# The middle stage of an FFT long convolution: pairs of frequency groups on the two halves of the TensorE array

## The chip, the cores and the metric

The kernel runs on one core of one Trainium2 chip. The metric is the device time of one execution in microseconds. Before the change it was 375.13 us, the median of 3 runs (375.03 to 375.66).

## The reference, cut to what matters

Two sequence layers over 2048 steps and 1024 channels are computed and put side by side in one bf16 output of 2048 x 2048.

```
# A: a gated long convolution
kv  = shift_conv4(k, shift_k) * v                     # 4 taps, per channel
y   = irfft(rfft(kv, 4096) * rfft(ssm_k, 4096))[:2048] + kv * ssm_D
a   = q * y
# B: a diagonal complex state space layer
Bu  = x @ B_bar.T ;  h_t = Lam_bar * h_(t-1) + Bu_t   # 1024 complex states
b   = 2 * Re(h @ C.T) + x * Dskip
out = concat([a, b], -1)
```

The change is in A alone, in the product of the two spectra and the transforms on either side of it.

## The kernel before

**Layer A in three stages.** The 4096-point transform is split into 16 residues `n2` of the step number, a 128-point transform over the rest, and a 16-point transform across the residues.

Stage 1 makes `kv` for each `n2` on VectorE (`kvm`, `kva`, `kvb`, `kvc`), transforms it with the constant `F1t` (task `am`, L573), copies it out on ScalarE (`ae`, L580) and stores it into the DRAM tensor `Ys_kv` (`ast`). The filter takes the same way: transposes (`hT`, L595), `hm` (L612), `he` (L618), `hst` (L625), into `Ys_h`.

Stage 2 handles 32 groups of 4 frequencies; a load brings two groups (`lh` from `Ys_h`, `lk` from `Ys_kv`; a pair is called `gq`, a group in it `gi`). One group fills 128 partitions: real or imaginary part x 16 residues x 4 frequencies. Its steps, each over two halves `w` of the 1024 channels, are

- `sh`, `sk` (L642): one 128x128 matmul of 512 columns each, with the constant `W2` of this group; the result has the real part in partitions 0 to 63 and the imaginary part in 64 to 127;
- `she` (L650) and `ske` (L656): ScalarE copies out of PSUM into `hab[:, 0, :]` and `x16`;
- `sw` (L661, L662): two DMAs from SBUF to SBUF, one on SyncE's queue and one on GpSimd's, that write into `hab[:, 1, :]` the same values with the halves of the partitions exchanged;
- `pr` (L667): one VectorE multiply of 2048 elements in each partition, `x16` by both parts of `hab`;
- `sa` (L676): two 128x128 matmuls that add up in one PSUM bank (with the constants `Wa`, `Wb`), `sae` (L683): the copy out, and `vst` (L685): the store of a pair into the DRAM tensor `Vs`.

Stage 3 loads each residue of `Vs` (`vl`), transforms back with `Gt` (`a3`, L702), copies out (`a3e`, L708), multiplies by q (`qm`, L712) and stores (`ost`, L714). A residue holds rows of all groups, so no `vl` can run before the last `vst`.

**Layer B** runs beside it in 16 chunks of 128 steps: `U` (L462, 128 matmuls of 128 columns in each chunk), `ue` (L464), two rotations, a scan and a carry on VectorE (`r1` to `r4`, `sc`, `rc`, `cm`, `ca`), then `y` (L517, with the skip term at L522) and `ye` (L528).

**The order** is written out by hand in the string `ORDER`: a list of words, each a task with its numbers and the buffers that it takes (`p` a PSUM bank of eight, `a`, `b`, `m`, `w` buffers in SBUF). Each engine and each DMA queue executes its instructions in the order of this list, so a wait holds up what stands behind it on the same engine. The tasks of both layers are mixed in it, and PSUM has no bank that one task owns.

Of the kernel before, what the change touches and what calls it, by code (L numbers as in the profile page):

```python
# [22 lines left out]
NG = 32  # L23


def a_constants():
# [32 lines left out]
    W3 = np.stack([W2.reshape(128, NG, 128), Wa.reshape(128, NG, 128), Wb.reshape(128, NG, 128)], axis=2)  # L59
# [7 lines left out]
ld_w:a0a1 wb.0:p0 wb.3:p1 wbe.3 cl.2.0:b0 bl.2.1:b1 wb.2:p2 ld_par par_T:p3 bl.3.0:b2 p32 exp1 dve2 wb.6:p4 exp2 wbe.2 wbe.6 wb.1:p1 dve3 sm_pre sin0  # L67
tabA1:a0a2a3a4 cT.2.0:p3 bl.1.1:b3 bT.1.1:p2 bc.1.1 bl.0.0:b4 bT.0.0:p4 wbe.1 wbe.0 bT.2.1:p1 bc.0.0 bT.3.0:p0 bc.3.0 bl.0.1:b5 bT.0.1:p5 bc.0.1
bl.3.1:b6 wb.7:p4 cc.2.0 bl.1.0:b7 bT.1.0:p6 x.1:b8 bT.3.1:p7 bc.1.0 wb.4:p0 U.1.0.0:a5p5 wbe.4 x.3:b9 U.3.0.0:a6p3 bl.2.0:b0 bT.2.0:p6 dd U.3.0.1
x.0:b10 wb.5:p0 U.0.0.0:a7p2 wbe.7 bc.2.1 bc.2.0 bc.3.1 U.1.1.0:p6 U.1.1.1 U.1.0.1 U.0.1.0:p7 U.3.1.0:p1 U.0.0.1 wbe.5 sin1 tabA2 sin2 par_rest eo  # L70
kp.-1 kp.0 kvm.1:m0 ue.1.0 kp.1 kvm.2:m1 U.0.1.1 kva.1 U.3.1.1 ue.3.1 ue.1.1 bl.4.1:b5 ue.0.0 x.2:b2 U.2.1.0:p0 bT.4.1:p5 bc.4.1 bl.4.0:b6 bT.4.0:p1
bc.4.0 stt kvb.1:b6 kva.2 bl.5.1:b7 bl.7.0:b0 bT.5.1:p6 bT.7.0:p2 bl.5.0:b1 bT.5.0:p4 bc.5.0 U.2.0.0:a1p5 U.2.0.1 kp.-2 ue.0.1 ue.2.0 bl.6.0:b4
bT.6.0:p4 bc.7.0 kvm.0:m0 bc.6.0 bc.5.1 U.0.2.0:p7 x.4:b3 U.4.0.0:a4p5 bl.6.1:b11 bT.6.1:p2 cl.3.1:b12 bc.6.1 bl.7.1:b13 U.1.2.0:p1 x.5:b14 U.0.2.1
ue.0.2 kvb.2:b11 kva.0 bT.7.1:p6 bc.7.1 vp.0:a8 z2 cT.3.1:p2 cc.3.1 ld_F cl.3.0:b0 z1 U.0.3.0:p4 U.0.3.1 cl.1.1:b1 ld_G U.1.2.1 ue.0.3 U.1.3.0:p6
U.1.3.1 cT.3.0:p2 kvm.3:m1 ue.1.2 vp.1:a9 U.2.1.1 kvb.0:b12 ue.3.0 kvc.0 am.0.0:p7 ae.0.0:b0 U.4.0.1 ue.1.3 ue.4.0 am.0.1:p1 cc.3.0 kva.3 cl.2.1:b7
cT.2.1:p3 kvc.2 kvb.3:b13 am.2.1:p7 am.2.0:p4 ae.2.0:b7 ae.2.1 U.2.2.0:p6 r1.0:m0 r2.0:a0 cT.1.1:p5 U.2.3.0:p2 ae.0.1 cc.1.1 am.0.2:p4 ae.0.2:b1
am.0.3:p7 ue.2.1 ae.0.3 hl.1.0:a3 U.2.2.1 U.3.2.0:p1 ue.2.2 kvc.1 am.1.3:p4 am.1.2:p0 ae.1.2:b12 ast.0.1 U.3.3.0:p5 cl.1.0:b4 cT.1.0:p6 U.3.3.1 kvc.3
cc.2.1 ae.1.3 ue.3.3 am.2.3:p3 hl.0.0:a10 am.2.2:p0 ae.2.2:b4 U.3.2.1 ue.3.2 ae.2.3 sc.0.1 sc.0.0 hl.0.1:a2 hT.0.2:p5 U.2.3.1 hc.0.2:b11 ue.2.3
U.4.2.0:p1 hm.0.2.0:p3 he.0.2.0:b1 ast.2.0 cc.1.0 cl.0.0:b5 cx.7.1 hl.1.1:a7 hT.1.1:p5 r1.1:m0 cT.0.0:p2 ast.0.0 hc.1.1:b5 am.1.0:p0 cm.0 cx.5.0
r2.1:a9 hT.0.0:p3 hc.0.0:b0 U.4.2.1 ue.4.2 hT.1.0:p6 ast.1.1 hm.0.2.1:p5 hc.1.0:b12 ast.2.1 hm.0.2.2:p4 hm.0.2.3:p7 he.0.2.1 he.0.2.2:b11 U.4.3.0:p3  # L80
U.4.3.1 ue.4.3 cx.6.0 am.1.1:p6 cl.0.1:b7 cT.0.1:p5 cc.0.1 U.5.2.0:p4 ca.0 rc.1 r3.0:m1 sc.1.0 U.5.0.0:a5p3 sc.1.1 U.5.2.1 cm.1 r3.1:m0 ld_sd hd.0
hd.1 r4.1 cc.0.0 ae.1.0:b7 ae.1.1 U.5.0.1 ue.5.0 hst.0.2.0 hm.1.0.2:p6 he.1.0.2:b6 r4.0 hm.1.0.0:p0 ue.5.2 hT.0.3:p2 hm.1.0.1:p5 hc.0.3:b1 hm.1.0.3:p3
he.1.0.3 ca.1 he.1.0.0:b12 he.1.0.1 hl.2.1:a8 U.5.3.0:p1 r1.2:m0 y.1.0.0:p4 hm.0.3.0:p2 he.0.3.0:b4 ast.1.0 r2.2:a1 rc.2 sc.2.1 r1.3:m0 hst.1.0.1
hst.1.0.0 sc.2.0 hm.0.0.3:p3 U.5.3.1 ue.5.3 hm.0.3.1:p5 hm.0.0.2:p0 he.0.0.2:b7 y.1.0.1 hm.1.1.2:p1 he.0.0.3 he.0.2.3 hm.1.1.1:p0 hst.0.0.1 kp.2
kvm.4:m1 hT.0.1:p2 hm.0.0.1:p3 cm.2 hm.0.0.0:p7 he.0.0.0:b0 lw.0:w0 he.0.0.1 y.0.0.0:p6 he.1.1.2:b6 cx.6.1 hm.1.1.3:p7 r2.3:a6 he.1.1.3 hst.1.1.1
hst.0.0.0 ca.2 r3.2:m0 y.0.0.1 he.0.3.1 hm.1.1.0:p1 he.1.1.0:b5 he.1.1.1 hc.0.1:b12 y.0.0.2 hT.1.2:p5 kva.4 kvb.4:b0 kvm.5:m1 hm.0.3.2:p1 he.0.3.2:b7
hT.1.3:p7 hm.0.3.3:p0 he.0.3.3 hst.0.3.1 y.0.0.3 am.3.2:p1 hst.0.2.1 cx.4.1 cx.7.0 cx.4.0 cx.5.1 y.1.1.0:p2 hm.0.1.0:p0 hst.1.1.0 y.1.1.1 hc.1.2:b1
hm.1.2.3:p5 hst.0.3.0 he.0.1.0:b6 y.1.1.2 y.1.0.2 y.1.0.3 ye.1.0:b8 y.1.1.3 ye.1.1 hl.3.0:a2 yst.1 vp.2:a10 rc.3 hm.1.2.2:p0 he.1.2.2:b7 he.1.2.3 r4.2
hc.1.3:b11 am.3.3:p3 ae.3.2:b5 hst.1.2.1 y.0.1.0:p4 y.0.1.1 y.0.1.2 ye.0.0:b10 y.0.1.3 ye.0.1 kvc.4 ae.3.3 ast.3.1 hm.0.1.2:p6 hl.2.0:a3 hm.0.1.1:p1
he.0.1.1 hst.0.1.0 hm.1.3.2:p7 he.1.3.2:b4 hm.1.3.0:p5 he.1.3.0:b8 hm.1.3.3:p0 hm.1.2.1:p4 sc.3.0 hm.1.3.1:p2 kp.3 he.1.3.1 y.2.0.0:p3 hT.2.0:p1  # L90
hc.2.0:b11 kvm.6:m0 he.0.1.2:b7 hm.0.1.3:p5 he.0.1.3 he.1.3.3 hst.1.3.1 y.2.1.0:p7 am.3.1:p2 am.4.0:p1 y.2.1.1 ae.4.0:b12 y.2.1.2 am.3.0:p1 am.4.1:p0
ae.3.0:b5 U.4.1.0:p5 ae.3.1 kp.4 kva.5 hm.1.2.0:p1 hd.2 hm.2.0.1:p6 hm.2.0.2:p2 hst.0.1.1 U.4.1.1 ue.4.1 kvb.5:b13 ast.3.0 y.2.0.1 y.2.0.2 yst.0
hT.2.1:p5 y.2.0.3 lw.1:w1 sc.3.1 cm.3 ae.4.1 ast.4.0 he.2.0.2:b1 kvc.5 am.5.2:p2 he.1.2.0:b2 he.1.2.1 hst.1.2.0 r3.3:m1 hc.2.1:b4 ae.5.2:b7 hst.1.3.0
ca.3 r4.3 vp.3:a7 hm.2.0.3:p4 he.2.0.3 hst.2.0.1 kva.6 am.4.2:p1 hm.2.0.0:p0 ye.2.0:b11 y.2.1.3 ye.2.1 he.2.0.0:b10 am.4.3:p2 ae.4.2:b0 ae.4.3
hT.2.3:p4 hc.2.3:b12 he.2.0.1 hl.3.1:a9 hT.3.0:p3 hc.3.0:b2 am.5.0:p7 ae.5.0:b5 ast.4.1 am.5.1:p5 ae.5.1 ast.5.0 r1.4:m1 am.5.3:p0 ae.5.3 ast.5.1
kvb.6:b13 y.3.0.0:p1 y.3.0.1 hm.2.3.0:p4 vp.5:a0 hm.2.3.2:p6 he.2.3.2:b8 y.3.1.0:p2 y.3.1.1 r2.4:a4 x.6:b6 hst.2.0.0 hm.2.3.1:p5 he.2.3.0:b1 he.2.3.1
hT.3.2:p0 hd.3 hm.3.0.2:p6 rc.4 hm.3.0.3:p7 y.3.0.2 kvc.6 am.6.0:p5 hc.3.2:b9 hm.3.0.0:p4 he.3.0.2:b0 he.3.0.3 vp.4:a10 hm.2.3.3:p0 he.2.3.3 hst.2.3.0
hst.2.3.1 hm.3.0.1:p3 he.3.0.0:b2 he.3.0.1 am.6.2:p6 ae.6.2:b12 kvm.7:m1 kva.7 vp.6:a1 y.3.0.3 kvm.8:m0 hT.3.1:p0 am.6.3:p4 ae.6.3 kp.5 am.6.1:p7
hc.3.1:b7 kvb.7:b13 hm.2.1.3:p3 y.3.1.2 y.3.1.3 hm.2.1.2:p0 ye.3.0:b10 ye.3.1 hst.3.0.1 hT.2.2:p4 U.5.1.0:p1 hm.3.2.0:p2 yst.2 ast.6.1 ae.6.0:b1
ae.6.1 ast.6.0 sc.4.0 he.2.1.2:b5 he.2.1.3 vp.7:a6 hm.2.1.1:p5 hm.2.1.0:p7 hst.3.0.0 U.5.1.1 ue.5.1 U.6.0.0:a3p3 U.6.0.1 hm.3.2.1:p1 kvc.7 am.7.3:p0  # L100
he.2.1.0:b4 he.2.1.1 he.3.2.0:b8 ue.6.0 hst.2.1.1 am.7.2:p5 hm.3.2.3:p7 hc.2.2:b0 hst.2.1.0 sc.4.1 r3.4:m1 U.6.1.0:p2 U.6.1.1 he.3.2.1 hst.3.2.0 kva.8
ae.7.2:b12 ae.7.3 ast.7.1 hm.2.2.0:p1 hm.3.2.2:p4 am.7.0:p5 ae.7.0:b1 am.7.1:p3 ae.7.1 ast.7.0 hT.3.3:p6 he.3.2.2:b13 he.3.2.3 hm.3.1.2:p0 he.2.2.0:b9
hst.3.2.1 U.6.2.0:p5 kp.6 kvb.8:b11 hc.3.3:b2 yst.3 ue.6.1 cm.4 r4.4 y.4.0.0:p3 y.4.1.0:p7 hm.3.3.3:p1 kvc.8 am.8.3:p6 hm.3.3.2:p4 he.3.3.2:b4
am.8.2:p2 ae.8.2:b8 y.4.1.1 hm.2.2.1:p4 he.2.2.1 hst.2.2.0 U.6.2.1 he.3.3.3 ae.8.3 hm.2.2.2:p2 he.2.2.2:b1 hm.2.2.3:p4 he.2.2.3 hst.2.2.1 hm.3.1.3:p1
he.3.1.2:b13 he.3.1.3 y.4.1.2 hm.3.3.0:p6 he.3.3.0:b0 U.6.3.0:p2 ue.6.2 hm.3.3.1:p0 hm.3.1.0:p4 he.3.1.0:b10 hm.3.1.1:p1 he.3.1.1 kvm.9:m1 kvm.10:m0
kva.9 kvb.9:b12 U.6.3.1 hst.3.3.1 ue.6.3 he.3.3.1 lw.2:w2 hst.3.3.0 kva.10 ca.4 y.4.0.1 y.4.0.2 y.4.0.3 ye.4.0:b3 kvc.9 am.9.1:p0 am.9.2:p2 r1.5:m1
ast.8.1 x.9:b5 U.9.2.0:p1 am.8.0:p3 ae.8.0:b1 U.9.0.0:a5p4 U.9.0.1 ue.9.0 y.4.1.3 ye.4.1 am.8.1:p3 kvb.10:b9 r2.5:a10 hst.3.1.1 kvc.10 am.10.3:p5
kvm.13:m1 am.10.0:p4 am.10.2:p6 hst.3.1.0 U.9.3.0:p7 yst.4 ae.8.1 ast.8.0 ae.10.0:b11 U.9.3.1 ue.9.3 U.9.2.1 kp.7 kvm.11:m0 ae.10.2:b13 ae.10.3 kva.13
ue.9.2 x.8:b2 U.8.0.0:a4p4 kva.11 kvb.13:b10 U.8.2.0:p6 kvc.13 am.13.2:p1 ae.13.2:b8 am.13.0:p5 ae.9.2:b3 U.8.2.1 ue.8.2 x.11:b7 ae.13.0:b1 kvm.12:m1
am.9.3:p1 ae.9.3 kva.12 ast.9.1 am.10.1:p7 kvb.11:b9 ae.10.1 U.8.1.0:p3 am.13.3:p6 kvb.12:b0 kvc.11 ast.10.0 am.9.0:p2 am.13.1:p5 ae.13.1 ae.13.3  # L110
ast.13.1 x.7:b4 U.7.0.0:a2p1 lh.1:a9 U.7.1.0:p7 U.7.1.1 kvc.12 am.12.0:p6 am.12.3:p5 ae.9.0:b10 ae.9.1 U.8.0.1 ast.9.0 ast.10.1 ae.12.0:b12 ue.7.1
# [65 lines left out]
def full_kernel(ctx, tc, A_q, A_k, A_v, A_shift_k, A_ssm_k, A_ssm_D, B_x, B_Lre, B_Lim, B_Bre, B_Bim,  # L177
# [3 lines left out]
    nc = tc.nc  # L181
    P = 128
# [445 lines left out]
    def lw(gq):  # L628
        st["w", gq] = rtile(ring, "w", "wts", [P, GC, 3, P])
        spd(st["w", gq][:], W3v[:, gq * GC:(gq + 1) * GC, :, :])  # L630
# [15 lines left out]
    def she(g, w):  # L646
        if w == 0:
            st["hab", g] = k4("hab", [P, 2, D])
# [132 lines left out]
```

## Time and profile before

| | |
|---|---|
| median of 3 runs | 375.13 us |
| profiled execution, whole / its span | 374.92 us / 372.7 us |
| busy TensorE / VectorE / ScalarE / GpSimd | 352.9 / 328.2 / 280.5 / 110.5 us |
| DMA | 101.38 MB, 272 GB/s on the mean |
| `sw`: DMAs on SyncE's queue, on GpSimd's | 32 + 32 of 128 KB, 3.9 and 4.0 us from issue to landing |
| granted TensorE clock | 1.00 in nearly all of the span |

The span runs from the first to the last instruction on the core; 2.2 us of the profiled execution lie outside it. Busy time of TensorE counts a matmul from its start to its modelled end, and matmuls overlap in the array; the distance from one start to the next says what each one costs. About 1 in 80 matmul records is missing from this trace (3486 of 3529 are there), which shows as a double distance in some places.

### The profile page before, as it was taken

The numbers are of one execution on the slowest core, as the hardware profiler recorded it, in microseconds if no ns is written. First come the engines' busy times: TensorE is split into PE (matmuls) and PEld (weight loads), VectorE is DVE, ScalarE is ACT, GpSimd is POOL, SyncE is SP. The second block draws the span as 40 slices with busy tenths as digits, with TensorE's granted clock in tenths as the row PEclk, the third lists the DMA queues.
The fourth block names the chain that finished last, engine by engine and source line by source line (L and its number), as shares of the span: only waits on it lengthen the run. The fifth ranks groups of instructions, "written<-read, shape, count | busy, mean of one in ns | idle before, by whom it ended". The sixth has DMA issues, their size and how long they took to land.

```text
span 372.7 us, 8839 instructions
## 1 busy us (share of the span) xinstructions
PE 352.9 (95%) x3486; PEld 243.2 (65%) x3529; DVE 328.2 (88%) x335; ACT 280.5 (75%) x519; POOL 110.5 (30%) x188
## 2 busy tenths in 40 slices
PE   5999999998999889999999999999999999999894
PEld 3899999755666767878575557644574756646341
DVE  5999999999898989989999999989884989975960
ACT  4999999958789875878599869878878876155381
POOL 3000032584667676214111202202130232002134
PEclk9999999999999999999999999999999999999999
DMA  7999999899696789898899888897979899699656
GB/s 242 264 283 279 329 272 226 237 332 365 180 330 161 286 273 232 269 286 257 250 254 275 253 280 299 237 345 228 289 251 272 256 267 401 209 359 332 268 197 253
DMA packets 60100, 101.38 MB, mean 272 GB/s; under 512 B 31102, under 2 KB 33150, under 8 KB 60060
## 3 DMA queue, kind: packets, MB, share of 16 engines
q1 hardware_dynamic: 47868, 62.93, 60.1%
q0 software_dynamic: 12192, 37.90, 28.6%
q8 instruction: 27, 0.44, 0.5%
q14 instruction: 13, 0.11, 0.1%
HBM read 52.57 MB, written 33.55 MB: 231 GB/s over the span
## 4 chain that ended last, share of the span: by engine, by line
PE 69%; DMA 11%; ACT 6%; issue 6%; POOL 5%; DVE 1%; POOLq 0%; SPq 0%; ACTq 0%
PE ps_u L462 26%; PE ps_y L517 19%; PE ps_a L676 7%; PE ps_a L642 7%; DMA Ys_h<-ysbh 6%; POOL Ys_h L625 4%; DMA Ys_kv<-ysb 3%; PE ps_t L427 3%; PE ps_a L702 2%; PE ps_y L522 2%; ACT ot L708 2%; ACT ysb L580 1%; PE ps_a L573 1%; ACT ysbh L618 1%; PE ps_a L612 1%
## 5 line engine op out<-in xcount | busy, mean ns | idle before, releaser
L462 PEld LDWEIGHTS <-BT 128*128 128x128 bf16 x2048 | 120.2, 98 | 13.0 <-issue 1.5
L462 PE MATMUL ps_u<-xT,BT 128*128 128x128 bf16 x2048 | 126.9, 219 | 0.5
L517 PE MATMUL ps_y<-CT,h 128*128 128x512 bf16 x490 | 124.8, 379 | 0.7
L517 PEld LDWEIGHTS <-h 128*128 128x128 bf16 x512 | 45.8, 98 | 44.7 <-issue 0.7
L493 DVE TENSOR_TENSOR_SCAN h<-rtab,h 128x1024 bf16<-128x1024 f32 x32 | 71.9, 2279 | 0.2
L625 POOL DMA_DIRECT2D Ys_h<-ysbh x64 | 46.3, 725 | 26.8 <-ACT ysbh L618 23.1
L464 ACT CAST u<-ps_u 128x512 bf16<-128x512 f32 x64 | 38.3, 616 | 18.0 <-PE ps_u L462 17.4
L667 DVE TENSOR_TENSOR hab<-x,hab 128x2048 bf16<-128x2048 bf16 x32 | 38.4, 1221 | 11.7 <-ACT x L656 9.5
L650 ACT CAST hab<-ps_a 128x512 bf16<-128x512 f32 x64 | 35.9, 618 | 8.7 <-PE ps_a L642 8.4
L683 ACT CAST vsb<-ps_a 128x512 bf16<-128x512 f32 x64 | 35.3, 616 | 9.2 <-PE ps_a L676 6.9
L580 ACT CAST ysb<-ps_a 128x512 bf16<-128x512 f32 x64 | 36.0, 633 | 6.6 <-PE ps_a L573 3.3
L656 ACT CAST x<-ps_a 128x512 bf16<-128x512 f32 x64 | 37.0, 630 | 4.1 <-PE ps_a L642 4.1
L582 POOL DMA_DIRECT2D Ys_kv<-ysb x32 | 17.5, 550 | 74.5 <-ACT ysb L580 74.4
L618 ACT CAST ysbh<-ps_a 128x512 bf16<-128x512 f32 x64 | 34.6, 612 | 6.2 <-DMA Ys_h<-ysbh 3.7
L474 DVE TENSOR_TENSOR mt<-u,Z 128x4096 bf16<-128x4096 bf16 x16 | 36.4, 2282 | 2.8 <-ACT u L464 2.8
L474 DVE TENSOR_TENSOR mt<-h,Z 128x4096 bf16<-128x4096 bf16 x16 | 36.5, 2284 | 0.1
L528 ACT CAST yo<-ps_y 128x512 bf16<-128x512 f32 x32 | 18.9, 609 | 21.5 <-PE ps_y L517 18.0
L676 PE MATMUL ps_a<-hab,wts 128*128 128x512 bf16 x125 | 32.5, 379 | 0.2
L662 POOL DMA_DIRECT2D hab<-hab x32 | 16.9, 529 | 52.4 <-ACT hab L650 35.6
L553 DVE TENSOR_TENSOR mt<-kring,wbc 128x4096 bf16<-128x4096 bf16 (+3 forms) x16 | 30.0, 1883 | 0.1
L522 PE MATMUL ps_y<-Dd,xT 128*128 128x128 bf16 x128 | 28.0, 219 | 0.4
L612 PE MATMUL ps_a<-hT,F1t 128*128 128x256 bf16 x128 | 20.2, 272 | 2.4 <-ACT ysbh L618 1.1
(109 smaller groups left out, 420.9 us busy)
## 6 DMA issues: line engine op xcount, KB each, us to landing
Ys_kv<-ysb POOLq DMA_DIRECT2D x32, 256.0 KB, 4.0
Ys_h<-ysbh POOLq DMA_DIRECT2D x64, 128.0 KB, 4.2
l2h<-Ys_h SPq DMA_DIRECT2D x16, 512.0 KB, 5.3
l2k<-Ys_kv SPq DMA_DIRECT2D x16, 512.0 KB, 4.8
Vs<-vsb POOLq DMA_DIRECT2D x16, 512.0 KB, 5.0
vv<-Vs SPq DMA_DIRECT2D x32, 256.0 KB, 5.2
kring<-in_A_k_dram SPq DMA_DIRECT2D x8, 512.0 KB, 6.1
v<-in_A_v_dram SPq DMA_DIRECT2D x8, 512.0 KB, 4.3
```

The lines of the kernel that those rows point to most:

```text
L462: nc.tensor.matmul(pu[:, w, jl, :], BT[:, 2 * jp + jl, w, d, :], xT[:, d, :], start=(d == 0), stop=(d == ND - 1))
L464: E["ue"] = lambda i, jp: nc.scalar.copy(st["u", i][:, :, 2 * jp:2 * jp + 2, :], st["pu", i, jp][:])
L474: nc.vector.tensor_mul(m, s_, win(Z))
L493: nc.vector.tensor_tensor_scan(gf, rt1, gf, 0.0, ALU.mult, ALU.add)
L517: nc.tensor.matmul(py[:], h[:, 1 - w, j, :], CT[:, j, w, dh * 512:(dh + 1) * 512], start=(j == 0 and w == 0), stop=(j == NJ - 1 and w == 1))
L580: nc.scalar.copy(st["ysb", n2, cc][:, dh * 512:(dh + 1) * 512], st["pa", n2, w][:])
L618: nc.scalar.copy(st["yh", qd, n4, w // 2][:, :, w % 2, :], st["pa", qd, n4, w][:].rearrange("p (c d) -> p c d", c=2))
L625: gpd(Ys_h[cc, n0:n0 + 2, :, qd * DQ:(qd + 1) * DQ].rearrange("n k d -> k n d"), t_[:, cc, :, :])
L650: nc.scalar.copy(st["hab", g][:, 0, cols], pt[:])
L656: nc.scalar.copy(st["x16", g][:, w * 512:(w + 1) * 512], st["ps", "l2k", g, w][:])
L667: nc.vector.tensor_mul(hab[:], st["x16", g][:].unsqueeze(1).to_broadcast([P, 2, D]), hab[:])
L676: nc.tensor.matmul(pt[:], st["w", gq][:, gi, 1 + a, :], hab[:, a, w * 512:(w + 1) * 512], start=(a == 0), stop=(a == 1))
```

## The change

A pair of groups is now handled together. The weights of the forward transform are cut into 64 columns for the real and 64 for the imaginary part (`cc`), and the two groups of the pair go to the two halves of the partitions of one PSUM bank. Real and imaginary part then lie in the free dimension of the same partitions (`hh[:, cc, :]`), so every product of the complex multiply is made in place: `pr` multiplies the real part of x by both parts of h, then the imaginary part by both. The DMAs of `sw` are gone. The inverse transform takes 64 partitions of one group at a time, four products for each output, and the two groups write two banks.

```
-    W3 = np.stack([W2..., Wa..., Wb...], axis=2)                # [128, 32, 3, 128]
+    W3 = np.concatenate([W2.reshape(128, NG // 2, 2, 128), half(wa), half(-wa), half(wb)], axis=2)
...
-        st["w", gq] = rtile(ring, "w", "wts", [P, GC, 3, P])
+        st["w", gq] = rtile(ring, "w", "wts", [P, 5, P])
...
-    def s2(nm, g, w):
-        gq, gi = divmod(g, GC)
-        st["ps", nm, g, w] = ptile("ps_a", [P, 512])
-        nc.tensor.matmul(st["ps", nm, g, w][:], st["w", gq][:, gi, 0, :], st[nm, gq][:, gi, w * 512:(w + 1) * 512], start=True, stop=True)
+    def s2(nm, gq, cc, w):
+        pt = ptile("ps_a", [P, 512])
+        st["ps", nm, gq, cc, w] = pt
+        for gi in range(GC):
+            nc.tensor.matmul(pt[64 * gi:64 * gi + 64, :], st["w", gq][:, gi, 64 * cc:64 * cc + 64], st[nm, gq][:, gi, w * 512:(w + 1) * 512], start=True, stop=True)
...
-        spd(hab[0:64, 1, :], hab[64:128, 0, :])
-        gpd(hab[64:128, 1, :], hab[0:64, 0, :])
...
-        nc.vector.tensor_mul(hab[:], st["x16", g][:].unsqueeze(1).to_broadcast([P, 2, D]), hab[:])
+        if cc == 0:
+            st["pp", gq, 0] = k4("pp", [P, 2, D])
+            st["pp", gq, 1] = st["hh", gq]
+        nc.vector.tensor_mul(st["pp", gq, cc][:], st["xx", gq, cc][:].unsqueeze(1).to_broadcast([P, 2, D]), st["hh", gq][:])
...
-        for a in range(2):
-            nc.tensor.matmul(pt[:], st["w", gq][:, gi, 1 + a, :], hab[:, a, w * 512:(w + 1) * 512], start=(a == 0), stop=(a == 1))
+        for a in range(2):
+            wi = (2, 4, 4, 3)[2 * h + a]
+            for gi in range(GC):
+                rows = slice(64 * gi, 64 * gi + 64)
+                nc.tensor.matmul(st["ps", "v", gq, w][gi][:], st["w", gq][rows, wi, :], st["pp", gq, h][rows, a, w * 512:(w + 1) * 512],
+                                 start=(h == 0 and a == 0), stop=(h == 1 and a == 1))
```

The string `ORDER` is replaced by another one from its first word to its last, in which both layers stand in a new mixture. In it the half-array matmuls of several pairs stand together: 512 of them in 22 stretches that hold nothing of full size. For example, where stage 2 begins:

```
U.8.3.0:p4 U.8.3.1 ... sh.2.0.0:p6 she.2.0.0:a8 lh.0:a9 sh.0.0.0:p3 she.0.0.0:a11 sc.5.1 sh.2.0.1:p1 sh.0.0.1:p2 sh.1.0.0:p7 sh.1.1.1:p4
ast.11.1 x.10:b13 sh.2.1.1:p0 sh.0.1.1:p6 she.1.0.0:a12 sh.2.1.0:p3 ... U.11.2.0:p7
```

## The prediction

> **What bounds the kernel now.** First the head of the page: the span, and busy time by engine.
>
> ```profile
> span 372.7 us, 8839 instructions
> PE 352.9 (95%) x3486; PEld 243.2 (65%) x3529; DVE 328.2 (88%) x335; ACT 280.5 (75%) x519; POOL 110.5 (30%) x188
> ```
>
> TensorE's 95% could flatter it, since matmuls overlap. So next the timeline of TensorE alone, in a quiet stretch of stage 2 (start, length, instructions):
>
> ```profile
> 289.31 1.24 PE L517 MATMUL ps_y<-CT,h 128*128 128x512 bf16 x5
> 290.39 1.03 PE L642 MATMUL ps_a<-l2h,wts 128*128 128x512 bf16 x4
> 292.12 1.06 PE L462 MATMUL ps_u<-xT,BT 128*128 128x128 bf16 x16
> ```
>
> One matmul of 512 columns is listed in the groups with 379 ns, so five in 1.24 us start (1.24 - 0.379) / 4 = 0.216 us apart; sixteen of 128 columns (219 ns each) start (1.06 - 0.219) / 15 = 0.056 us apart. The same reading gives 0.109 for 256 columns. With these distances the whole program costs TensorE: U 2048 x 0.056 = 114.7; y 512 x 0.216 = 110.6 and its skip term 128 x 0.056 = 7.2; sh and sk 128 x 0.216 and sa 128 x 0.216 = 55.3; am and a3 64 x 0.216 each = 27.6; hm 128 x 0.109 = 14.0; 320 transposes at 0.056 to 0.062 = 18.7; the eight of L413 about 3.1. Sum 351.2 us. The first matmul starts at 4.5 and the last ends at 367.3 us, so the span is 4.5 + 351.2 + 11.6 of waits and slow starts + 5.4 after the last matmul. TensorE sets the time; nothing else has to be cheap, only early enough.
>
> Third, where the 11.6 us lie: the table by stretch (us; busy TensorE, its weight loads, VectorE, ScalarE, GpSimd, clock, DMA share, GB/s), cut at the stages, and the list of what TensorE waited for.
>
> ```profile
> 4.00:77.00 73.00, 71.59 (x1048) 64.41 (x1053) 69.81 (x111) 66.91 (x113) 12.47 (x19) 1.00 1.05 276
> 77.00:138.00 61.00, 56.03 (x490) 37.79 (x496) 57.81 (x53) 48.04 (x86) 39.61 (x59) 1.00 0.84 275
> 172.00:330.00 158.00, 156.90 (x1315) 96.39 (x1334) 144.80 (x115) 118.13 (x232) 30.11 (x56) 1.00 0.89 277
> 330.00:373.00 43.00, 35.32 (x211) 17.88 (x212) 23.99 (x27) 21.14 (x40) 11.27 (x21) 0.99 0.75 270
> ```
>
> ```profile
> PE ps_a L702 <- ACT ot L708: 1.8, 1, 1.8
> PE ps_a L573 <- ACT ysb L580: 1.4, 2, 0.9
> PE ps_a L612 <- ACT ysbh L618: 1.1, 1, 1.1
> PE ps_a L612 <- ACT yo L528: 1.0, 1, 1.0
> PE ps_a L573 <- DVE mt L560: 0.8, 1, 0.8
> ```
>
> With three smaller ones these waits make 7.4 us (the 4.5 before the first matmul apart); the rest is the slow clock of the first 6 us of matmuls. They belong to stage 1 and the end. The stretch 172 to 330, in which nearly all of stage 2 runs, has 156.9 busy of 158, and no wait of TensorE there is listed. That is the main reading: the change works where TensorE waits for nobody.
>
> **What is removed.** 64 DMAs of 128 KB and their issues: 32 x 0.467 = 14.9 us on SyncE's queue, 32 x 0.529 = 16.9 us on GpSimd's, 8.4 of 101 MB. Who waited for them, and for the step before:
>
> ```profile
> POOL hab L662 <- ACT hab L650: 35.6, 19, 3.4
> DVE hab L667 <- ACT x L656: 9.5, 5, 4.0
> DVE hab L667 <- DMA hab<-hab: 2.1, 2, 1.2
> ```
>
> The exchange cost VectorE 2.1 us of waiting and TensorE none, since U and y lay over it. GpSimd's 35.6 us held up the stores behind it on its queue, again under TensorE's work. Gain on the path: 0. The weights shrink from 192 to 160 KB a load, under the same cover: 0. What is late next for pr is ScalarE (the 9.5 us row).
>
> **What is unchanged.** she, ske, sae: 64 copies of about 0.62 us each; pr 32 x 1.22 us. Each stays as wide as it was. But pr now needs six copies of a pair, not four copies of one group; and sa holds two PSUM banks from its first half (h = 0) to its second and to their copies. An sa that waits holds back the U and y behind it.
>
> **What is added, on TensorE.** 256 full matmuls become 512 halves, in 256 pairs on disjoint halves of the array. No row of this trace shows a pair. The near end is 0.216 us a pair (each half still streams 512 columns, so a gain is excluded); the far end is two full ones, 0.432, 256 x 0.216 = 55.3 us more. I take the near end, because the distances above follow the columns streamed alone (56, 109, 216 ns) and the two halves share no cell of the array; plus 5 ns for the second issue, which is what lies between a load and its matmul in the next view (11.80 and 11.81): 256 x 0.005 = 1.3 us. [...]
>
> The loads double too, to 512 of half size. The row 172 to 330 has 156.9 us of matmuls and 96.4 us of loads in 158 us, all of full height: loads lie under running matmuls of the same rows. So I cost them at 0; unhidden, 256 column-half loads at 0.056 (a load and a matmul of 128 columns fit into that) would be 14.3 us. [...]
>
> Changing the form of the array has a price in this trace: L413 uses one row (a 32-row form) between full ones.
>
> ```profile
> 11.43 0.44 PE L427 MATMUL ps_t<-ident,ld 128*128 128x128 bf16 x5
> 11.80 0.09 PEld L413 LDWEIGHTS <-ones 1*128 1x128 bf16 x1
> 11.81 0.39 PE L413 MATMUL ps_a<-hk,ones 1*128 1x512 bf16 x1
> 12.12 0.28 PE L427 MATMUL ps_t<-ident,ld 128*128 128x128 bf16 x2
> ```
>
> The fifth L427 starts at 11.43 + 4 x 0.056 = 11.65, L413 0.15 later instead of 0.056; the next one 0.32 after L413 instead of 0.216. Six such places read singly give 95 to 102 ns. The program before changes form 7 times, the new one 49 times (rows, columns, full): 42 x 0.098 = 4.1 us, in a stretch without slack.
>
> **The new order.** It can move TensorE's waits both ways. Counting in both orders, over the 130 us of TensorE work of stage 2, how often a PSUM bank is taken again within 1.3 us of TensorE work after its last matmul: 23 of 212 before, 40 of 212 after; in the part of stage 1 where the waits are, 11 of 114 and 10 of 110. The half-array stretches fill banks faster (0.216 us each) than ScalarE empties them (0.62). Bounds: -7.4 us (all listed waits go) and +10.5 (17 further tight places at one copy of 0.62). I take 0, since 23 tight places cost nothing in stage 2 before.
>
> Sum: 4.1 + 1.3 = 5.4 us. Span 372.7 + 5.4 = 378.1, profiled execution 374.92 + 5.4 = 380.3, median 375.13 + 5.4 = **380.5 us**. A measurement of this kernel can tell about 0.2% (0.75 us) from no change.
>
> **Rivals.** (1) *The order wins back more than the forms cost*: faster. TensorE waits 7.4 us in stage 1 and the end, where the new order differs too, and fewer DMAs can free ScalarE's buffers earlier (5 waits, 3.7 us, for Ys_h stores). If all go, 380.5 - 7.4 = 373.1; without the 1.3 for pairs 371.8. It decides from 6.2 us regained. Against it: those waits are for stage 1, which the removed DMAs don't touch. Chance 0.23; another 0.06 that both cancel within 0.2%.
> (2) *Loads are not hidden, or stretches starve on PSUM banks*: 380.5 + 14.3 = 394.8, or 380.5 + 10.5 = 391. For it: 40 tight places. Chance 0.09.
> (3) *The halves don't run side by side*, so that the change doesn't do what it says: 380.5 + 55.3 - 1.3 = 434.5. One kind alone (columns or rows): about 407. Chance 0.09.
>
> **The numbers.** My forecast, pairs side by side and forms paid for, has 0.53 and its own range 376 to 386. Faster 0.23, same 0.06, slower 0.53 + 0.09 + 0.09 = 0.71. The range runs from 371.5 (rival 1 at its full price) to 395 (rival 2), and leaves out rival 3 and little else.
>
> **What would show it.** Right: in L642 and L676 two starts some ns apart, then 0.216 us to the next pair; about 0.1 us lost at each change of form; sum of TensorE's distances near 357; DVE's and POOL's hab rows gone, and the stretch of stage 2 longer by some 5 us. Wrong: starts 0.216 apart inside a pair (rival 3); starts of pairs 0.27 apart, or TensorE waiting for ACT copies of L650 to L683 (rival 2); TensorE's listed waits below 2 us (rival 1). A changed span with unchanged waits and 351 us of distances would refute the price of the forms.

## The result, and the profile after

The changed kernel takes 390.47 us (median of 4 runs, 386.12 to 394.29) where the kernel before takes 375.39 (375.03 to 377.81) beside it: a ratio of 1.035, with a 95% interval of 1.024 to 1.045. It is slower by some 15 us. The ratio leaves out the longest run, which is over 1.5% above the fastest. The profiled execution took 391.46 us, its span is 389.7 (before: 374.92 and 372.7), and the 17.0 us between the spans are what has to be found.

The head of its page answers to the first lines shown of before:

```profile
span 389.7 us, 9237 instructions
PE 363.3 (93%) x3785; PEld 244.9 (63%) x3785; DVE 332.3 (85%) x335; ACT 278.1 (71%) x519; POOL 93.0 (24%) x156
```

TensorE has 256 matmuls more (the page of before lacks the 43 records that are missing there) and 10.4 us more of busy time, while its share fell from 95 to 93%. Part of the loss is therefore work and part is time without work. GpSimd has its 32 instructions less.

The timeline of TensorE alone, where a stretch of half-array matmuls begins (start, length, instructions):

```profile
194.19 0.59 PE L524 MATMUL ps_y<-CT,h 128*128 128x512 bf16 x2
194.72 0.41 PE L650 MATMUL ps_a<-l2h,wts 128*64 128x512 bf16 x2
194.96 0.38 PE L650 MATMUL ps_a<-l2k,wts 128*64 128x512 bf16 x2
195.17 0.38 PE L650 MATMUL ps_a<-l2h,wts 128*64 128x512 bf16 x2
195.39 1.25 PE L650 MATMUL ps_a<-l2k,wts 128*64 128x512 bf16 x10
196.56 0.62 PE L469 MATMUL ps_u<-xT,BT 128*128 128x128 bf16 x8
```

Each of the first three L650 rows is a pair. Two matmuls of 0.38 us that ran one behind the other would show 0.216 + 0.38 = 0.6 us, as the L524 row of two does; these show 0.38 to 0.41. Single records give starts of 194.715 and 194.718, so 3 ns lie inside the pair, and the next pair follows after 0.24, then 0.21 and 0.22 us. Ten in 1.25 us are five pairs 0.216 apart. The two column halves do run at once.

The groups by shape (busy, mean ns) give 384 and 377 ns for one half-array matmul, as for a full one of 512 columns; only the distance between starts tells that two share it:

```profile
L650 PE MATMUL ps_a<-l2h,wts 128*64 128x512 bf16 x128 | 20.3, 384 | 0.0
L680 PE MATMUL ps_a<-pp,wts 64*128 64x512 bf16 x128 | 19.7, 377 | 0.0
```

Then the table by stretch, cut at the stages of the new order (us; busy TensorE, its loads, VectorE, ScalarE, GpSimd, clock, DMA share, GB/s):

```profile
5.00:77.00 72.00, 67.25 (x992) 60.10 (x992) 65.05 (x108) 61.00 (x103) 8.85 (x15) 1.00 1.04 264
77.00:150.00 73.00, 70.15 (x663) 48.50 (x662) 68.55 (x59) 54.98 (x99) 44.13 (x65) 1.00 0.80 247
150.00:183.00 33.00, 30.32 (x447) 26.41 (x445) 28.29 (x30) 24.61 (x49) 13.14 (x22) 1.00 0.73 208
183.00:320.00 137.00, 136.03 (x1275) 77.19 (x1272) 127.40 (x100) 110.81 (x222) 11.43 (x22) 1.00 0.67 219
320.00:390.00 70.00, 59.58 (x422) 32.61 (x420) 41.10 (x39) 25.43 (x49) 12.87 (x24) 0.95 0.73 254
```

The stretch of stage 2, 183 to 320, is as tight as before by this measure. The idle time has grown in stage 1, and there in the first row: 4.75 us against 1.41 before in the like row. The next two rows have 5.5 us, and before it was 5.9 from 77 to 172: 4.97 in the row 77 to 138 shown ahead and 0.9 in the one behind it:

```profile
138.00:172.00 34.00, 33.10 (x431) 26.66 (x436) 29.84 (x30) 25.00 (x50) 13.84 (x23) 1.00 0.89 251
```

The list of what TensorE waited for in the changed kernel names the waits:

```profile
PE ps_a L619 <- ACT hT L607: 3.6, 2, 3.3
PE ps_a L580 <- DVE mt L567: 2.7, 1, 2.7
PE ps_a L619 <- ACT ysb L587: 1.5, 1, 1.5
PE ps_a L580 <- ACT ysbh L625: 0.7, 1, 0.7
...
PE ps_a L680 <- DVE hh L670: 0.5, 2, 0.4
```

The chain of waits leads back from the 3.3 us wait to a store:

```profile
52.58 9.14 DMA Ys_kv<-ysb
...
61.80 0.42 ACT ysb L587
...
63.36 1.83 ACT hT L607 x2
...
65.73 0.27 PE ps_a L619
```

The buffer `ysb` came free when a store that took 9.14 us had landed. ScalarE's copies stood behind that, hT behind them, and the matmuls of L619 last.

The last place is the end. The table by stretch once more, for the last 13.7 us:

```profile
376.00:380.00 4.00, 4.00 (x22) 1.85 (x20) 1.90 (x3) 1.20 (x3) 2.36 (x5) 1.00 0.87 319
380.00:384.40 4.40, 0.35 (x2) 0.00 (x0) 0.00 (x0) 0.59 (x1) 0.54 (x1) 0.89 0.47 175
384.40:389.70 5.30, 0.00 (x0) 0.00 (x0) 0.00 (x0) 0.00 (x0) 0.00 (x0) 0.50 0.00 0
```

For 5.3 us no engine works and no DMA moves a byte. What fills 4.5 of them is an instruction of GpSimd's sequencer, which busy time leaves out: the closing DRAIN. Its row in the view by source line (least, median and largest ns, first and last start), before and then after:

```profile
L776 POOLq DRAIN  x3: 51/99/3701, 368.2 to 372.4; - x3
```

```profile
L780 POOLq DRAIN  x3: 51/112/7653, 381.2 to 389.4; - x3
```

Before, this DRAIN ended 0.7 us after the last store had landed (371.9 and 371.2 us) and the span 1.5 us after; now it is 5.3 us (388.9 and 383.6) and 6.1.

Measured from start to start of TensorE's matmuls, the 17.0 us divide as follows.

| | before | after | more |
|---|---|---|---|
| span's start to first matmul | 4.5 | 5.1 | 0.6 |
| first matmul to last matmul | 362.4 | 374.9 | 12.5 |
| of it: 44 changes of form at half-array matmuls | | | 4.2 |
| of it: pairs over 0.216 us | | | 0.7 |
| of it: waits inside half-array stretches | | | 3.2 |
| of it: waits at matmuls of full size | 9.7 | 13.7 | 4.0 |
| last matmul to the span's end | 5.8 | 9.7 | 4.0 |

The middle rows leave 0.4 us of slow clock and roundings. The 44 changes are 19 stretches entered and left, with six turns between column and row halves inside them; the stretches are 19 in the trace, and not the 22 that are named with the change.

### The profile page after: what moved, and what is told of

The parts are those of the page before. It is cut to its first block, busy times and chain, and to the rows that moved or that the text cites. A ratio compares the mean times of both kernels' runs of the same rounds, so it can differ in the third digit from the quotient of the medians.

```text
span 389.7 us, 9237 instructions
## 1 busy us (share of the span) xinstructions
PE 363.3 (93%) x3785; PEld 244.9 (63%) x3785; DVE 332.3 (85%) x335; ACT 278.1 (71%) x519; POOL 93.0 (24%) x156
## 3 DMA queue, kind: packets, MB, share of 16 engines
q0 software_dynamic: 10656, 33.71, 24.0%
## 4 chain that ended last, share of the span: by engine, by line
PE 51%; ACT 14%; issue 12%; DVE 10%; DMA 9%; POOL 2%; POOLq 0%; ACTq 0%; DVEq 0%
PE ps_y L524 18%; PE ps_u L469 15%; PE ps_a L680 4%; PE ps_a L650 4%; DMA Ys_h<-ysbh 4%; ACT hh L657 3%; PE ps_a L619 3%; PE ps_a L580 3%; ACT xx L663 3%; DVE mt L560 2%; DMA Ys_kv<-ysb 2%; ACT vsb L687 2%; DMA out_dram<-ot 2%; DVE mt L567 2%; POOL out_dram L718 1%
## 5 line engine op out<-in xcount | busy, mean ns | idle before, releaser
L524 PE MATMUL ps_y<-CT,h 128*128 128x512 bf16 x512 | 127.0, 379 | 0.3 <-ACT ot L712 0.2
L469 PE MATMUL ps_u<-xT,BT 128*128 128x128 bf16 x2048 | 124.7, 219 | 0.6 <-ACT BT L445 0.3
L469 PEld LDWEIGHTS <-BT 128*128 128x128 bf16 x2048 | 118.4, 98 | 10.5 <-issue 4.1
L524 PEld LDWEIGHTS <-h 128*128 128x128 bf16 x512 | 45.2, 98 | 45.0 <-issue 2.4
L625 ACT CAST ysbh<-ps_a 128x512 bf16<-128x512 f32 x64 | 35.6, 616 | 16.9 <-PE ps_a L619 6.6
L689 POOL DMA_DIRECT2D Vs<-vsb x16 | 8.5, 534 | 122.8 <-ACT vsb L687 96.7
L657 ACT CAST hh<-ps_a 128x512 bf16<-128x512 f32 x64 | 36.0, 649 | 2.3 <-PE ps_a L650 2.2
L687 ACT CAST vsb<-ps_a 128x512 bf16<-128x512 f32 x64 | 34.2, 694 | 3.3 <-PE ps_a L680 3.3
L663 ACT CAST xx<-ps_a 128x512 bf16<-128x512 f32 x64 | 35.8, 660 | 0.6 <-PE ps_a L650 0.6
L619 PE MATMUL ps_a<-hT,F1t 128*128 128x256 bf16 x128 | 20.5, 272 | 5.6 <-ACT hT L607 3.6
L712 ACT CAST ot<-ps_a 128x512 bf16<-128x512 f32 x32 | 17.4, 606 | 10.7 <-PE ps_a L706 6.3
L670 DVE TENSOR_TENSOR pp<-xx,hh 128x2048 bf16<-128x2048 bf16 x16 | 19.4, 1220 | 6.0 <-ACT xx L663 3.5
```

The costliest lines, as they stand in the source:

```text
L469: nc.tensor.matmul(pu[:, w, jl, :], BT[:, 2 * jp + jl, w, d, :], xT[:, d, :], start=(d == 0), stop=(d == ND - 1))
L524: nc.tensor.matmul(py[:], h[:, 1 - w, j, :], CT[:, j, w, dh * 512:(dh + 1) * 512], start=(j == 0 and w == 0), stop=(j == NJ - 1 and w == 1))
L625: nc.scalar.copy(st["yh", qd, n4, w // 2][:, :, w % 2, :], st["pa", qd, n4, w][:].rearrange("p (c d) -> p c d", c=2))
L657: nc.scalar.copy(st["hh", gq][:, cc, w * 512:(w + 1) * 512], st["ps", "l2h", gq, cc, w][:])
L663: nc.scalar.copy(st["xx", gq, cc][:, w * 512:(w + 1) * 512], st["ps", "l2k", gq, cc, w][:])
L687: nc.scalar.copy(st["vsb", gq][:, gi, w * 512:(w + 1) * 512], st["ps", "v", gq, w][gi][:])
```

## The experiments

Three theories stood after the first look. By the first (A in the expectations), the loss has two sources: the half-array matmuls, and an order in which TensorE waits for others; without the halves 4 to 6 us come back. By the second (B), the half-array matmuls are all of it, and without them the time comes back to some 376 us. By the third (C), their price lies in waits that would be there anyway, and nothing comes back. A further question was what the removed exchange is worth by itself. The chip's runs of the kernel before had medians of 376.32, 374.58 and 376.22 us in the three sets that follow; each ratio is against its own set.

### The change again, and the change with full matmuls

The changed kernel was run once more in the first set.

> The changed kernel once more, as the base of the others. Four runs so far lay between 386.1 and 394.3 us, those of the kernel before within 0.7 us but for one. Theory A (the new order leaves TensorE more waits for stores to land, and a heavier burst of stores at the end): the median stays near 390 and the spread of several us comes back, since the landing of stores varies. Theory B (a fixed price of the half-array matmuls): the same median, and a spread near that of the kernel before.

It took 392.18 us (389.14 to 397.14), ratio 1.038 [1.030, 1.047]: the same median within the noise, and the same wide spread.

Then the 512 halves became 256 matmuls of full size at the same places of the same order, with the same copies and products around them. The two groups are mixed in the sums, so the values are others.

```
-        for gi in range(GC):
-            nc.tensor.matmul(pt[64 * gi:64 * gi + 64, :], st["w", gq][:, gi, 64 * cc:64 * cc + 64], st[nm, gq][:, gi, ...], start=True, stop=True)
+        nc.tensor.matmul(pt[:], st["w", gq][:, cc, :], st[nm, gq][:, cc, ...], start=True, stop=True)
...
-            for gi in range(GC):
-                ...
+            nc.tensor.matmul(st["ps", "v", gq, w][a][:], st["w", gq][:, wi, :], st["pp", gq, h][:, a, ...], start=(h == 0), stop=(h == 1))
```

> The changed kernel with its order, banks, copies and DMAs, but each pair of half-array matmuls is one full 128x128 matmul of 512 columns (half of the products of the middle stage are left out). 256 matmuls instead of 512, form changes 5 instead of 49. Theory A: the price of the forms alone comes back, 44 x 0.095 = 4.2 us, and some 0.7 us of the pairs, so 4 to 6 us below the changed kernel, near 385; the rest stays with the order. Theory B: all the loss is in the half-array matmuls, so near 376. Theory C: the drains lie in waits that would be there anyway, so within 1 us of the changed kernel.

It took 390.34 us (388.7 to 393.37), ratio 1.037 [1.030, 1.044]. Changes of form and pairs, 4.9 us of TensorE's time by the table above, are gone, and the median came down by 1.8 us beside the run of the changed kernel, which the spreads don't tell from nothing. The second theory falls. Between the first and the third these medians don't decide: the first's own figure, 385 us, was missed by 5. In the two profiled executions the way from first to last matmul fell from 374.9 to 372.7 us, so 2.2 of the 4.9 us came through. Part of the rest is found again as waiting: at 50 places this kernel's TensorE waits 18.2 us, against 16.9 in the changed kernel (13.7 + 3.2).

```profile
PE ps_a L580 <- ACT ysbh L625: 2.5, 2, 1.6
PE ps_a L619 <- ACT hT L607: 2.2, 2, 2.0
PE ps_a L619 <- ACT ysb L587: 1.9, 2, 1.6
PE ps_a L677 <- DVE hh L669: 1.5, 4, 0.6
```

The table by stretch of the same kernel shows what one such wait can bring after it (the clock stands behind the five engines and ahead of the DMA share):

```profile
60.00:62.40 2.40, 0.49 (x9) 0.37 (x7) 0.69 (x3) 1.39 (x3) 1.09 (x2) 1.00 1.23 223
62.80:66.20 3.40, 3.40 (x25) 2.60 (x24) 3.33 (x4) 2.77 (x6) 0.35 (x1) 0.51 1.11 327
66.20:70.00 3.80, 3.80 (x36) 2.60 (x35) 3.77 (x3) 1.43 (x4) 1.11 (x2) 0.99 0.70 272
```

TensorE was busy 0.49 of 2.4 us, and for the 3.4 us after that its clock was 0.51. That is 25 matmuls where the following 3.8 us hold 36, and costs some 1.7 us over the wait itself (an estimate, 3.4 x 0.49). The profiled execution of the changed kernel has no such window, so this one is the greater part of what the full matmuls did not bring in these two traces, and it does not come in every execution.

The repeat of the changed kernel shows this best, for its profiled execution is the one of 397.14 us. It has three such windows, behind waits near 62, 123 and 158 us. This is the first of them, and the stretch ahead of it:

```profile
60.83:64.24 3.41, 1.15 (x21) 1.03 (x19) 1.20 (x4) 2.69 (x5) 1.09 (x2) 1.00 1.27 224
64.24:67.66 3.42, 3.42 (x25) 2.77 (x25) 3.35 (x5) 2.54 (x5) 0.00 (x0) 0.50 1.00 350
```

Three windows cost some 5 us (3 x 1.7 by the same estimate), and from first to last matmul this execution takes 6.3 us more than the other one of the same kernel (381.2 against 374.9).

### Column pairs alone, in the old order

The kernel before, with each of its forward matmuls cut into two column halves. The order, the DMAs and all else stay. This is a place where TensorE has no slack.

```
-        nc.tensor.matmul(st["ps", nm, g, w][:], st["w", gq][:, gi, 0, :], ...)
+        for cc in range(2):
+            nc.tensor.matmul(st["ps", nm, g, w][64 * cc:64 * cc + 64, :], st["w", gq][:, gi, 0, 64 * cc:64 * cc + 64], ...)
```

> The kernel before with its own order; only each matmul of sh and sk becomes two of 64 columns on the two column halves, into the same bank, with the same result. 128 more matmuls, form changes 129 instead of 7. Theory A: 122 x 0.095 = 11.6 us, pairs at 3 ns each: 387 us. If the halves ran one after the other, 128 x 0.216 = 27.6 us on top: 414. Theory C (drains swallowed): 375 to 377.

It took 389.64 us (387.6 to 390.68), ratio 1.034 [1.028, 1.040]: 13.3 us more, with 122 more changes of form. The timeline of TensorE, where full and half matmuls alternate:

```profile
204.64 0.41 PE L643 MATMUL ps_a<-l2k,wts 128*64 128x512 bf16 x2
204.88 0.38 PE L643 MATMUL ps_a<-l2h,wts 128*64 128x512 bf16 x2
205.19 0.60 PE L677 MATMUL ps_a<-hab,wts 128*128 128x512 bf16 x2
205.73 0.41 PE L643 MATMUL ps_a<-l2k,wts 128*64 128x512 bf16 x2
```

From the second pair to the full matmul it is 0.31 us instead of 0.216, and from the second full one (205.19 + 0.216) to the next pair 0.32. Over the whole trace 61 entries cost 93 ns each and 61 exits 109, together 12.3 us, and the pairs 0.9. So here the price comes through to the time, 13.2 us of 13.3. It also shows that the mixture in the changed kernel, whose pairs stand together, is what keeps the forms at 4.2 us.

### The exchange taken out alone

The kernel before without the 64 DMAs of `sw`. Both products of `pr` use the unexchanged halves, and so does `sa`; the exchanged halves are left out of the computation.

```
-        spd(hab[0:64, 1, :], hab[64:128, 0, :])
-        gpd(hab[64:128, 1, :], hab[0:64, 0, :])
...
-        nc.vector.tensor_mul(hab[:], st["x16", g][:].unsqueeze(1).to_broadcast([P, 2, D]), hab[:])
+        for _ in range(2):
+            nc.vector.tensor_mul(hab[:, 0, :], st["x16", g][:], hab[:, 0, :])
```

> The kernel before without the 64 DMAs that exchange the halves; the products that need exchanged halves are left out, and pr is two multiplies of 1024 elements on the same half (2 x 0.69 instead of 1.22 us, some 5 us more of VectorE in all, which has slack in that stretch). Theory A: the exchange lay under TensorE's work, so 375.1 within 1 us. Rival: the DMAs and their queue time slowed the stores and loads of the end, so 2 us or more below, at 373 or less.

It took 379.45 us (379.32 to 383.51), ratio 1.011 [1.002, 1.019]. Taking work out made the kernel some 3 us slower, where no change was expected and the rival had it faster. From the first matmul to the last it takes 363.5 us (before: 362.4); the end took 9.6 instead of 5.8. Its table by stretch and its closing DRAIN:

```profile
371.20:377.70 6.50, 0.00 (x0) 0.00 (x0) 0.00 (x0) 0.00 (x0) 0.00 (x0) 0.56 0.00 0
```

```profile
L776 POOLq DRAIN  x3: 51/107/7572, 369.3 to 377.4; - x3
```

The end of the changed kernel is there, without its order, its pairs or its math.

### Which queue it is, and in which direction

In the kernel before, only the half of the exchange that GpSimd issues was given to SyncE. All 64 DMAs and all bytes remain.

```
-        gpd(hab[64:128, 1, :], hab[0:64, 0, :])
+        spd(hab[64:128, 1, :], hab[0:64, 0, :])
```

> The kernel before with the same work and result; the half of the exchange that GpSimd's queue issued goes to SyncE's queue (149 on GpSimd's, 232 on SyncE's). Theory D: the tail grows from 5.8 to 9.7 us, so some 379 us. Rival: the tail stays at 5.8 and the time within 1 us of before, unless SyncE's queue holds up loads, which would show as waits of TensorE.

It took 380.06 us (378.72 to 383.39, 10 runs), ratio 1.010 [1.006, 1.014], with a DRAIN of 7.572 us and 363.7 us from first to last matmul. So the longer end comes from what GpSimd's queue no longer issues, and costs what it did without the exchange.

If fewer DMAs on that queue make the DRAIN longer, 32 added ones should make it short again. The changed kernel got 32 reads of 32 bytes there, two behind each store of `Vs`.

```
+        for z in range(32 * gq, 32 * gq + 32, 16):
+            gpd(scr[0:1, z:z + 16], F1d.ap()[0:1, z % 256:z % 256 + 16])
```

> The changed kernel with the same work and result, and 32 DMAs of 32 bytes more on GpSimd's queue, two behind each store of the middle stage: 181 DMAs there, as before, not 149. In the runs so far every kernel with 149 had 9.6 to 10.8 us from the last matmul's start to the end, every one with 181 had 5.8. Theory D (GpSimd's last drain takes longer when its queue has issued fewer DMAs): the tail falls to 5.8 and the median by 3.9 us, to about 387 to 388. Rival (the pile of output stores, or the missing bytes, make the tail): unchanged within 1 us.

It took 395.61 us (393.68 to 398.67), ratio 1.049 [1.040, 1.058]. The DRAIN became longer still:

```profile
L786 POOLq DRAIN  x3: 51/112/10267, 385.8 to 396.6; - x3
```

The theory that a smaller number makes it longer fell with that. What the traces give is a table, and no rule for it. The packets are those of the software queue (GpSimd's) in the list of queues:

| GpSimd's DMAs | packets | closing DRAIN, us | kernels |
|---|---|---|---|
| 181 | 12192 | 3.70 to 3.74 | before, column pairs alone, one spliced order |
| 149 | 10656 | 7.57 to 7.65 | changed kernel, full matmuls, no exchange, half of it on SyncE, other orders |
| 181 | 11680 | 10.27 | 32 small reads added (two kernels) |

Within one row the DRAIN differs by less than 0.1 us between kernels with quite different orders. So in these kernels it goes with what the queue issued and not with the work around it; which property of that, these rows don't tell.

### Where the order loses

Four kernels were meant to find the part of the order that costs the rest. The two orders were joined at the first step of stage 2 or behind its last one, and buffers given out anew where the joint needed it (11 to 95 places).

```
-ORDER = <order of the changed kernel>
+ORDER = <order of before up to its first lh> + <what is left, in the changed order>                   # h1_front
+ORDER = <changed order up to its first lh> + <what is left, in the order of before>, in before's code  # h0_front
+ORDER = <changed order up to its last sae> + <what is left, in the order of before>                    # t1_end
+ORDER = <both joints of h1_front and t1_end>                                                           # ht_both
```

> The changed kernel, with the order of the kernel before up to the first load of the middle stage (725 words); then the words that remain in the new order. Buffer numbers are changed in 87 of 919 places where the old ones were still held. Theory A: TensorE's waits in that part go back from some 11 to some 7 us, so 4 us below the changed kernel, near 386, with a smaller spread. Theory B (half-array matmuls cost it all): near 390.

> The mirror of it: the kernel before (full matmuls, exchange by DMA), with the new order up to the first load of the middle stage (780 words), then its own; buffer numbers changed in 94 places. Theory A: the new front brings its waits along, 4 us or more above the kernel before, 379 or more, with a wider spread. Theory B: 375 to 376.

> The changed kernel in its own order up to the last copy of the middle stage; then the remaining words in the order of the kernel before (11 buffer numbers changed). Theory A: from the last matmul to the end it is 9.4 us in the changed kernel and 5.4 before, because stores of the output pile up; with the old ending some 4 us of that come back, near 386.5. Rival: the pile is set by when the middle stage ends and not by the order of the end, so within 1 us of the changed kernel.

> Old front and old ending together, the new middle with its half-array matmuls. Theory A: what is left over the kernel before is the forms, 4.2 us, the pairs, 0.7, and the 2.3 us of waits that stand inside the half-array stretches: 375 + 7 = 382. Theory B: near 390.

They took 402.71 (ratio 1.075 [1.067, 1.082]), 399.17 (1.065 [1.058, 1.071]), 403.29 (1.074 [1.067, 1.081]) and 413.11 us (1.100 [1.095, 1.106]). Every joint lost more than the change it was to explain: from first to last matmul it is 385.1 to 393.8 us against 362.4 and 374.9. The second one has none of the changed math and still lost 24.6 us. Three of the four expectations, 382 to 386.5 us, were missed, and their rivals with them; the one of h0_front, 379 or more, was met by 20 us that it had not meant. These four say nothing on the parts of the new order. They show that a cut through either order is dear: 24.6 us over the kernel before, and some 11 to 23 us over the changed kernel.

The last attempt went to the wait at 62 us. In the changed kernel, five transposing DMAs (L452) are issued between 48 and 59 us, while the store of 9.14 us was on its way. They were made into plain loads of the same size and number, which leaves C untransposed.

```
-    E["cx"] = lambda d, w: nc.sync.dma_start_transpose(CT[..., d * P:(d + 1) * P], Cv[w][d * P:(d + 1) * P, :])
+    E["cx"] = lambda d, w: spd(CT[..., d * P:(d + 1) * P], Cv[w][d * P:(d + 1) * P, :].rearrange("p (j i) -> p j i", i=P))
```

> The changed kernel, with the eight transposing loads of C in the first stage replaced by plain loads of the same size (that part of C is not transposed). Five of them run within 14 us in which two stores took 9.1 us to land, and TensorE then waited 3.5 us at 64. Theory A: these stores land in about 3.5 us, that wait goes, and with it the half clock that follows it in some executions: 3 to 5 us faster than the changed kernel, 386 to 388, and waits of TensorE fall by 3. Rival: the stores land late for another reason, or the time goes to the next wait: within 1.5 us of the changed kernel.

It took 390.28 us (387.63 to 392.75), ratio 1.037 [1.028, 1.045]. The wait there fell from 3.5 to 1.5 us, the stores still took 7.1 to 7.5 us to land, and other waits took its place:

```profile
PE ps_a L580 <- ACT ysbh L625: 3.3, 2, 2.7
PE ps_a L619 <- ACT ysb L587: 1.8, 1, 1.8
PE ps_a L706 <- ACT ot L712: 1.8, 1, 1.8
PE ps_a L619 <- ACT hT L607: 1.3, 1, 1.3
```

Behind the first matmul the waits in the whole list make 11.8 us in all, against 11.0 in the changed kernel, where 3 us less were expected. The transposes are thus not shown to be the reason for the slow store, and one wait less did not bring the time back. The same edit together with the 32 small reads:

> Both edits together: 32 tiny DMAs more, and plain loads instead of the eight transposing ones (that part of C is not transposed). Theories A and D add up: 391 - 3.9 - 4 = 383. If the plain loads give nothing: 387.

It took 393.93 us (391.53 to 396.69), ratio 1.047 [1.039, 1.055], with the DRAIN of 10.27 us again; what was hoped of both fell with the small reads.

## Why the prediction was right or wrong

The sign was right, and the time lies in the range; the size was not: 15 us more, where the sum had 5.4. The forecast's own range, 376 to 386 us, was missed. That the wide one holds the time is in part luck: its upper end was set for rival 2, and half of the loss came from places where no rival expected one. By its steps:

**Pairs.** Right. Column pairs start 3 ns apart and are 0.216 us from pair to pair. The price was 1.3 us in the sum and 0.7 in the trace (5 ns a column pair, 1 ns a row pair). Rival 3 is refuted.

**Loads.** Right at 0. A load of 64 columns takes 106 to 110 ns and runs under matmuls of the same rows: in the changed kernel one of 110 ns starts 2 ns after the start (195.386 us) of a matmul of 379 ns. One of 64 rows takes 92 to 96 ns. The pair distance of 0.216 us leaves no room for the 14.3 us of the estimate for loads that are not hidden, so this half of rival 2 falls.

**Changes of form.** Right: 4.2 us against 4.1, and 93 to 96 ns for entering against 98. There are 44 at half-array matmuls where 42 more were counted, since the new program has two fewer at one-row matmuls. The row of L413, one matmul of one row, was a good price for it. The column pairs in the old order confirm it at three times the number.

**The removed exchange, "Gain on the path: 0".** Half right. From first to last matmul its removal gains nothing (363.5 us against 362.4), as the profile of before said. But the step missed that GpSimd's queue ends in a DRAIN, and that with 32 DMAs less there it takes 7.57 us instead of 3.70. The runs without the exchange and with half of it on SyncE both cost 3 to 4 us and show it. In the profile of before only the 3.7 us DRAIN itself pointed there, and the page's busy time doesn't count it.

**"The new order. I take 0".** This is the step that failed, inside its bounds of -7.4 and +10.5. The waits grew by 7.2 us: 4.0 at matmuls of full size, mostly in stage 1, and 3.2 inside the half-array stretches. The second part is of the kind that the tight places were counted for, and smaller than 10.5. The first part the sum had no step for: it looked at PSUM banks, and the wait that grew most goes back to an SBUF buffer held by a store. Rival 1 had such waits in it, but only as something to win.

**The rivals.** What happened is rival 2's number (391) with half of its reason: stretches that wait for ScalarE's copies and VectorE's products cost 3.2 us, and not its 10.5. The rest came from stage 1 and from the end, where no rival expected a loss. Rival 1 is refuted: the order won nothing back.

**What stays open.** 5.4 us of the sum, 7.2 of waits and 4.0 of the end make 16.6; the measured terms are 4.9 + 7.2 + 4.0 + 0.6 + 0.4 = 17.1 of the span's 17.0. So the places are all known, but not why stage 1 waits more in the new order: the spliced orders and the plain loads did not settle it. The spread is settled in part, 386 to 394 us where the kernel before keeps within 3 beside it (and within 5.4 in the 13 runs of the last set). Windows of half clock behind a wait come in some executions of the changed kernel and not in others, none before the end of the one of 391.46 us and three in the one of 397.14; that they are all of the spread was not shown, and the runs that are shorter than 391 us have no trace. No kernel of these runs beats the one before.

## What to carry to other kernels

Matmuls that fill half of the array cost next to nothing over their streams here where two on opposite halves stand together (5 or 1 ns a pair), and 93 to 109 ns at each change of form; so group them, and count the changes. TensorE set the time, and the DMAs that lay under its work brought nothing when they went (363.5 us from first to last matmul against 362.4); what the queues do after the last matmul (a DRAIN of 3.7 to 10.3 us) has to be costed like any other stage. An order that is tuned as a whole is best taken as a unit: a saving inside it may not reach the time, as of 4.9 us saved here the medians show 1.8, which is within their spread, and a part spliced into another order told nothing of that part.

## What was not expected of the hardware

GpSimd's closing DRAIN took 3.7, 7.6 or 10.3 us by what its queue had issued, monotone neither in the number of DMAs nor in packets; with 10.3 us, the last 7.9 us of the span pass with no byte moved and every engine idle.

After a wait of TensorE of 2.2 to 3.1 us the granted clock was at half for one window of 3.4 us in the kernel with full matmuls (at 62.8 us) and three times in the one with small reads, at 63, 125 and 159 us. The changed kernel, with waits of 3.5 and 2.9 us, shows none of it in the profiled execution.

The traces show what goes with it. Within each of the 14, every change of the granted clock lies a whole number of 3.413 us from every other, to about a nanosecond (in the changed kernel's 109 of them are 372.05 us, in that of before 106 are 361.81), and where this grid begins differs between executions: the first full clock comes at 11.40 us in the changed kernel's trace and at 16.46 in its repeat's. What separates the cases here is the idle time inside one window of the grid, from the modelled end of a matmul to the next start. Of the 1492 windows at full clock in all traces, up to the last matmul, 17 were followed by half clock, and these hold 1.99 to 2.73 us of idle time; none of the others holds more than 1.93. In the changed kernel the longest wait lies across two windows, with 1.59 and 1.86 us of it, as the busy time of these two stretches shows:

```profile
59.19:62.60 3.41, 1.82 (x33) 1.70 (x31) 1.23 (x2) 0.80 (x2) 0.00 (x0) 1.00 1.15 287
62.60:66.02 3.42, 1.56 (x21) 1.38 (x21) 3.35 (x6) 3.42 (x6) 1.09 (x2) 1.00 1.06 265
```

In the repeat a shorter wait, 2.26 us, lies in one window, 60.83 to 64.24 as shown above, and the clock of the next 3.42 us was 0.50. None of the 17 windows was idle throughout: 2.0 us of the 3.4 were enough here.
